# Transposing q and x on TensorE in place of transposing transfers, in a linear-attention and GELU kernel

## The chip, the cores and the metric

The kernel runs on one core of one Trainium2 chip. The core has TensorE (PE, matmuls; its weight loads are listed as PEld), VectorE (DVE), ScalarE (ACT), GpSimd (POOL) and SyncE (SP), which here only issues transfers. The metric is device time in microseconds (us) of one execution, as the median of several runs. Matmuls write to PSUM, which is handed out in banks; everything else that the kernel keeps on the chip lies in SBUF.

## What is computed

For 8 batches, 8 heads, 576 rows and a head size of 64, a linear attention; then two matrix products with a GELU between them.

```python
phi = lambda t: np.where(t > 0, t, np.exp(t) - 1.0) + 1.0
q_p, k_p = phi(q), phi(k)                       # 8 x 8 x 576 x 64
kv = einsum('bhsd,bhse->bhde', k_p, v); z = sum(k_p, axis=2)
x = einsum('bhsd,bhde->bhse', q_p, kv) / (einsum('bhsd,bhd->bhs', q_p, z)[..., None] + 1e-6)
h = x.transpose(0, 2, 1, 3).reshape(4608, 512) @ w_in      # w_in 512 x 2048
out = gelu_tanh(h) @ w_out                                 # w_out 2048 x 512
```

All inputs and the output are fp32 in HBM; on the chip q, k and v become bf16, x, the weights and the GELU's result g fp16.

## The kernel before

**Groups.** The 4,608 rows are worked on in nine groups of 512, `iteration(j)` at line 1065. Group j, from 0 to 7, has the first 512 rows of batch j; group 8 has the remaining 64 rows of each of the eight batches. While group j's matrix products run, the attention of group j+1 is made and the inputs of later batches are mapped.

**Order by hand.** What is issued when is written out in nine lists of words, ORDER_A to ORDER_I (lines 1123 to 1182, group 0 to 8), which `iteration` reads from left to right. Each engine and each queue works through its own instructions in that order. The words:

- `p6` makes block 6 (128 of the 2,048 columns) of h as four plain matmuls of 128x512, and `g6` its GELU. `X`, `Y`, `Z`, `W` with a name are steps of a unit of seven products (`Quad`, line 989): four blocks of h made as seven products of half-size quarters (28 matmuls of 128x256, line 999) in place of eight (16 matmuls of 128x512, line 356). The other steps of a unit are copies and sums: `s` and `u` copy on ACT, `m` copies on DVE, `c` and `a` add on DVE, `g11` to `g22` are GELUs. A prime at a word takes the other of DVE and ACT for its copy. The units' first rows are FIRST_BLOCK = (0, 2, 4, 6) for X, Y, Z, W; X covers blocks 0, 1, 8 and 9.
- A unit needs sums of quarters of w_in (`sum_w_in`, line 956, words `!w0` to `!w3` for X, Y, Z, W; four DVE instructions each) and sums of quarters of x (`sum_x`, word `!xs`).
- `o1` to `o7` with `os`, `ou`, `oc11` and so on make the second product in the same way (line 784), and `S1` to `S4` sum quarters of g on DVE.
- `!lq:3`, `!lk:3`, `!lv:3` issue loads of batch 3 on SP; `!qe`, `!qx`, `!qm` and `!ke`, `!kx`, `!km` make phi of q and k (exp on ACT, the linear part and the minimum on DVE); `!re`, `!rx`, `!rm` do so for the rest rows; `!vc` casts v; `k3` makes kv of batch 3 (line 262).
- `n0` to `n3` make one chunk of 128 rows of the next group's x: matmuls of q's transpose with kv (line 278), then a reciprocal and a multiplication on DVE (lines 295 and 296).

**Transposes.** TensorE needs phi(q) and x with the contracted dimension on the partitions. In groups 0 and 1 both are transposed by TensorE: a transpose is a matmul of 128x128 with the data as weights and an identity as the moving operand, into a PSUM bank, and a copy moves it to SBUF (lines 410, 349, 516, with copies at 413, 350, 521). From batch 2 on, `least_q` (line 619) issues four transposing transfers on SP for each q behind its minimum, `transposed_x` (line 641) issues one for each x chunk behind its division, and `least_rest` (line 565) one for each of the four pieces of the rest rows: `nc.sync.dma_start_transpose`, SBUF to SBUF.

**Buffers.** The pool `pld` has seven load buffers. At the start they are taken by q, k and v of batch 0 and by four blocks of w_in; a later load waits on SP until the readers of an earlier one are done. In group 1 the words `!bq` and `!mq` take two of them for good (tiles A and B), which hold sums of w_out, the sums of w_in for X and W, and small pieces; group 2's `!br` takes one more for rows. Group 0 and group 1 use plain blocks only; group 2 makes two units (Y and Z) and eight plain blocks; groups 3 to 8 make four units. PSUM has a pool of six single banks (`ps_b`) and one pair.

**Around the start.** POOL makes identities, sets constants and casts most of the weights (lines 141 and 147); group 1's maps, transposes and kv are slotted into group 0 by `plan_second` (line 496), `maps` among them.

Of the kernel before, what the change touches and what calls it, by code (L numbers as in the profile page):

```python
# [17 lines left out]
def kernel(  # L18
# [9 lines left out]

# [6 lines left out]
    P = 128  # L39
# [40 lines left out]
    def bank(name, shape, dt=FP32):  # L80
        return ps_b.tile(shape, dt, name=name, tag="b")
# [3 lines left out]

# [65 lines left out]

    nc.scalar.preload_act_table_set("exp_and_others")
# [9 lines left out]
    for i in (2, 1, 3):  # L162
        load_w_in(i)
    load_w_out(0)
# [17 lines left out]

    warm = pg.tile([P, 512], BF16, name="warm", tag="g")
    nc.vector.memset(warm, 0.0)
    ident = pth.tile([P, P], BF16, name="ident")
    make_identity(nc, ident)
    vps = [pkv.tile([P, J * NP, E], BF16, name=f"vp{i}") for i in range(2)]
    ident_x = pth.tile([P, P], FP16, name="ident_x")
    t_sum = pth.tile([P, 3, KM // 2, MAIN // 2], FP16, name="t_sum")
    kvbds = [pkv.tile([P, NP, 2 * E], BF16, name=f"kvbd{b}") for b in range(B)]  # L190
    make_identity(nc, ident_x)
    for i in range(2):
        nc.gpsimd.memset(vps[i][:, :, D:E], 1.0)
    for t in kvbds:
        nc.gpsimd.memset(t, 0.0)

# [4 lines left out]

    phi, exps, own = {}, {}, {}
# [44 lines left out]

# [137 lines left out]
    def xt_chunk(j, c):  # L385
        return xts[j][:, :, P * c : P * (c + 1)]
# [5 lines left out]

# [90 lines left out]

# [12 lines left out]
    def plan_second():  # L496
# [3 lines left out]
        def maps():  # L500
            for n in "qk":
                exp_of(n, b)
            cast_w_out(2, nc.scalar.copy, slice(0, 2))
            linear_of("q", b)
            sum_w_out(slice(0, 1))
            linear_of("k", b)
            for n in "qk":
                least_of(n, b)
# [56 lines left out]
    def least_rest(m):  # L565
        least_of("qr", m)
        if m == 0:
            qts[B] = pt.tile([P, C, NP, P], BF16, name="qt")
        nc.sync.dma_start_transpose(
            out=qts[B][:, m], in_=phi["qr", m][:, 0].rearrange("p h d -> p (h d)")  # L570
        )
# [5 lines left out]
    def load_rests(i):  # L577
# [32 lines left out]
        "bq": lambda j: begin_sums(),  # L610
        "mq": lambda j: more_sums(),
# [7 lines left out]
    def least_q(b, cs=slice(0, C)):  # L619
        least_of("q", b, cs=cs)  # L620
        if b not in qts:
            qts[b] = pt.tile([P, C, NP, P], BF16, name="qt")
        for c in range(cs.start, cs.stop):
            nc.sync.dma_start_transpose(
                out=qts[b][:, c],
                in_=phi["q", b][:, c].rearrange("p h d -> p (h d)"),
            )
# [13 lines left out]
    def transposed_x(b, c, x):  # L641
        if b not in xts:
            xts[b] = pt.tile([P, NP, MAIN], FP16, name="xt")
        nc.sync.dma_start_transpose(out=xt_chunk(b, c), in_=x)

    x_parts = {}

    def attention_piece(b, c, in_banks=False):

        if b < B:  # L650
            return transposed_x(b, c, (nab_in_banks if in_banks else nab)(qts[b], b, c))
# [27 lines left out]
        transposed_x(b, c, x)  # L679
# [36 lines left out]


# [205 lines left out]
    FIRST_BLOCK = (0, 2, 4, 6)  # L923
    def sums_at(u, t):
        own["sums"][u] = t.rearrange("p (u n c) f -> p u n c f", u=1, c=KM // 2)
        own["w"][u] = own["sums"][u][:, 0]

    own["w"], own["sums"] = {}, {}
    for u in (1, 2):
        sums_at(u, w_near[:, u])  # L930

    def begin_sums():

        own["A"] = pld.tile([P, MM + 2, N2], FP16, name="w_sum", tag="ld")
        sums_at(3, own["A"][:, MM // 2 : MM])

    def more_sums():

        own["B"] = pld.tile([P, MM + 2, N2], FP16, name="w_more", tag="ld")
        own["qr", 0] = own["B"][:, MM:].rearrange("p a n -> p (a n)").bitcast(BF16)  # L940
        sums_at(0, own["B"][:, MM // 2 : MM])

# [122 lines left out]
    def iteration(j):  # L1065
# [10 lines left out]
        for word in ORDERS[j].split():  # L1076
# [27 lines left out]
            elif kind == "k":  # L1104
                kv_in_pair(int(name))
            elif kind == "S":
# [4 lines left out]
            elif kind == "!":  # L1111
                what, _, b = name.rstrip("'").partition(":")
                if what == "vc":
                    cast_v_of(int(b), name.endswith("'"))
                elif b:
                    prepare_of[what](int(b))
                else:
                    prepare[what](j)
# [5 lines left out]
        "p0 g0 p1 g1 p2 g2 p3 g3 p8 g8 p9 g9 p10 g10 p11 g11 !w1 p4 g4 p5 g5 p6 g6 p7 g7 p12 g12 "  # L1124
        "p13 g13 p14 g14 p15 g15 !w2 @15 o0:0-4 o1:0-4 o2:0-4 o3:0-4 o0:4-8 o1:4-8 o2:4-8 o3:4-8 "
        "@23 o0:8-10 o1:8-10 o2:8-10 o3:8-10 @27 o0:10-12 o1:10-12 @29 o2:10-12 o3:10-12 o0:12-16 "
        "@32 o1:12-16 @33 !qe:2 o2:12-16 @34 o3:12-16 @35"
    )
    ORDER_B = (
        "p0 !ke:2 p13 !lk:3 p1 !kx:2 !vc:2' !km:2 !t !qx:2 @2 p7 !qm:2 p2 g0 !bq !lv:3 !mq g1 g2 "  # L1130
        "p3 g3 k2 !a0 !a2 !a3 p6 p4 p5 p8 g4 p11 g5 !kxb:3 p9 g6 g7 T0-8 o1 os' g8 g9 p10 !qx:3 "
        "!kxa:3 g10 p12 o7 !lk:4 g11 p14 g12 g13 om S1:0-6 p15 S2:0-5 g14 g15 n1' o2 S1:6-8 "
        "S2:5-8 S4:0-6 n0 oc11' o6 !qe:3 n3' ou S4:6-8 !ke:3 n2 o5 oc22 !lq:4 !km:3 !vc:3 o4 oc21 "
        "o3 oc12' !qm:3 !ke:4 !xs !kx:4"
    )
    ORDER_C = (
        "!br k3 @1 Y1 Z1 !km:4 p6 Zs p0 !lk:5 !t g6 !lv:4 Z2 Zg11 Z6 p14 Z7 p8 Zu Z5 Zm g14 p7 g0 "
        "g8 Ys p15 !qx:4 Zc g7 Y6 Yu' Zg22 Y2 Yg11 Y7 Ym Z4 Za g15 n1 p1 g1 Y5 Yc Zg21 Y4 Ya Z3 "
        "Zg12 S1:4-8 n3 o1 Yg22 S2:4-8 p9 S1:0-1 S2:0-1 n2 Yg21 os g9 Y3 Yg12 S1:1-3 S1:3-4 "
        "S2:1-3 S2:3-4 S3:0-8 !qe:4 n0' o2 !lv:5 !qm:4 o6 oc11 ou o7 om o5 !kx:5 S4:0-8 oc22 "  # L1140
        "!ke:5 !vc:4 !xs o4 oc21 o3 !km:5 k4 oc12"
    )
    ORDER_D = (
        "!lq:5 !w0 Z1 X1 !t Y7 Y1 Xs X2 !w3 X7 @1 Ym' X6 Xg11 Ys n1 Xm' Y2 X4 Y6 Xu Xa X5 Yg11 Zs "
        "Xc Yu Xg21 n0 !lk:6 Y4 !vc:5' Z6 Zu X3 Xg12 Z2 Ya Y5 W1 Z7 Yc Zg11 Ws k5 Xg22 Zm Yg21 W6 "
        "Wu' Z5 Yg22 Y3 Yg12 !lv:6 Zc W7 Wm' W2 Z4 Za W5 Zg22 Z3 Wc W4 Wa n3 Wg11 Zg12 Zg21 o1 "
        "S1:0-6 Wg21 n2 os W3 Wg12 S2:0-6 !lq:6 Wg22 S1:6-8 S2:6-8 o2 !qe:5 S3:0-5 o6 S3:5-8 o7 "
        "S4:0-8 !qx:5 ou !qm:5 om !ke:6 oc11 o5 !lk:7 oc22 !vc:6 !kx:6 o4 o3 oc21 !xs oc12'"
    )
    ORDER_E = (  # L1150
        "X1 X7 Xm Xs Y7 !t X6 X2 Xg11 Xu' @1 Y1 Ym X4 X5 Ys Xa Xg21 Z1 Y2 Yg11 Zs !lr:0 Y4 Xc X3 "
        "!km:6 Y6 Yu n2 Z7 Xg12 Z6 Ya Z2 Zu Xg22 Yg21 n1 Zm W1 Z5 Y5 Yc Zc Zg11 Ws k6 Z4 Yg22 W7 "
        "Za Z3 Wm' Zg22 W6 Wu' n3 W4 Zg12 W2 Wg11 Wa Y3 W5 Wc Yg12 S1:0-6 S2:0-6 Zg21 Wg21 o1 os "
        "n0 Wg22 W3 Wg12 S1:6-8 S2:6-8 S3:0-8 !qx:6 o2 !lv:7 S4:0-8 !qe:6 o6 ou !lq:7 oc11 o7 om "
        "!xs o5 oc22 !re:0 o4 !re:1 !ke:7 !qm:6 oc21 !kx:7 o3 oc12'"
    )
    ORDER_F = (
        "!t !km:7 X1 Y1 Y7 !vc:7' Xs Ym' X6 X7 @1 X2 Xu Y4 Xm' !lr:1 X5 Xc X4 Xa Xg11 Ys k7 Y6 "
        "Yu' Y2 Xg22 Xg21 X3 Z1 Yg11 Zs !qx:7 Y5 W1 Yc Z2 Xg12 Ya Zg11 Z6 Zu Ws' Y3 Z7 Zm n1 Yg12 "
        "Z5 Yg22 W6 Wu S1:0-2 W7 Z4 W2 W5 Wm' Zc !rx:0 Zg22 Z3 Zg12 Wc Wg11 n0 Wg22 W4 S1:2-6 "  # L1160
        "S3:0-6 W3 Wg12 o1 os S1:6-8 S3:6-8 S2:0-8 n3 !qe:7 o7 om' o6 Wa Za Zg21 Yg21 ou' n2 o4 "
        "!qm:7 S4:0-6 o5 oc22 Wg21 o2 !rm:0 oc11 S4:6-8 o3 oc21 oc12 !xs"
    )
    ORDER_G = (
        "X1 n0 !rx:1 !rm:1 Xs Y7 Ym' X7 Xm' X2 X6 Xu' Xg11 Y1 Ys X4 Xa n2 X5 Y2 Z1 Xg21 Y6 Y4 "
        "Yg11 Zs W1 Xc Xg22 Yu' Ya !rx:2 X3 Xg12 Yg21 Y5 @1 Z6 Yc Z2 Z7 Zg11 Zu' Ws' Y3 Z5 Yg22 "
        "W7 Wm' W2 Wg11 Yg12 Zm Zc W6 Wu' W4 Zg22 Wa Z3 Zg12 Z4 W5 Za Zg21 Wc S1:0-6 o1 Wg21 "
        "S2:0-6 os n1 W3 Wg22 Wg12 S1:6-8 S2:6-8 S3:0-8 n3' o2 !rx:3 o6 o7 oc11' !re:2 ou S4:0-8 "
        "om o5 !re:3 !rm:2 oc22 o4 oc21 !rm:3 o3 !xs oc12' !t"
    )  # L1170
    ORDER_H = (
        "X1 Xs X7 Xm' n0' n1 X6 Xu X2 Xg11 X4 Y1 Xa X5 Y7 Xc Ys Y6 Xg21 Y2 Yg11 Yu' Z1 X3 W1 Zs "
        "Y5 Z6 Z2 Xg12 Ym Yc Y4 @1 Z7 Zu' Z5 Xg22 Zg11 Ya Y3 Ws W6 W2 Zm Yg21 Zc W7 Yg22 Wu' Wm "
        "Zg22 Wg11 Z3 Zg12 W5 Z4 Za Yg12 Zg21 Wc Wg22 W4 Wa S1:0-6 o1 os W3 Wg21 S2:0-6 Wg12 "
        "S1:6-8 S2:6-8 S3:0-8 n2 n3' o2 oc11 o6 ou o7 om o5 S4:0-8 o4 oc22 !xs o3 oc21 oc12'"
    )
    ORDER_I = (
        "X1 Y7 Ym X7 Xm Xs X2 Xg11 @1 X6 Y1 X4 Z1 Ys Y6 Xu' Xa Xg21 Y2 Y4 Yg11 Zs X5 Yu' Ya Y5 "
        "Yg21 Z7 Z2 Z6 W1 Xc Xg22 Zg11 Yc Y3 Yg22 Zu' X3 Ws' Z5 W6 Zm Zc Yg12 Wu W2 W7 W5 Wg11 Wm "
        "Zg22 Wc Xg12 Z4 Za Z3 Zg12 W4 Wa W3 Wg12 S1:0-6 S2:0-1 Wg22 o1 S1:6-8 S2:1-8 S3:0-8 o5 "  # L1180
        "Zg21 o6 Wg21 S4:0-8 o7 o2 o4 o3"
# [36 lines left out]
```

## Time and profile before

| what | value |
|---|---|
| median of 3 runs | 265.94 us (265.37 to 266.69) |
| the profiled execution | 266.18 us |
| its span, first to last instruction | 264.4 us |
| last matmuls | from 248.73 us on, 12.24 us |
| transposing transfers | 28 of x, 24 of q, 4 of the rest rows |
| median from issue to landing of these | x 2.3, q 4.1, rest 2.3 and 3.1 us |
| HBM read, written | 36.70 MB, 9.44 MB |

How to read what follows: a line by shape gives line, engine, operation, tiles and shape, then how often it ran, its busy time in us, the mean ns of one, and the idle time of its engine just before. A line of the timeline gives start and length in us, engine, line, operation and count; matmuls are pipelined, so a run's length is a little more than count times spacing. A line of waits gives who waited for whom: us in total, times, longest. A line of sums by stretches gives the stretch, its length and, for each engine, busy us and the number of instructions, then the granted clock, the DMA share and GB/s. Groups begin on PE at about 47.4 (group 1), 77 (group 2), 104, 130.4, 156.8, 183, 208.4 and 234.4 us (group 8).

### The profile page before, as it was taken

The numbers are of one execution on the slowest core, as the hardware profiler recorded it, in microseconds if no ns is written. First come the engines' busy times: TensorE is split into PE (matmuls) and PEld (weight loads), VectorE is DVE, ScalarE is ACT, GpSimd is POOL, SyncE is SP. The second block draws the span as 40 slices with busy tenths as digits, with TensorE's granted clock in tenths as the row PEclk, the third lists the DMA queues.
The fourth block names the chain that finished last, engine by engine and source line by source line (L and its number), as shares of the span: only waits on it lengthen the run. The fifth ranks groups of instructions, "written<-read, shape, count | busy, mean of one in ns | idle before, by whom it ended". The sixth has DMA issues, their size and how long they took to land. (4 is left out here: it accounts for less than half of the span.)

```text
span 264.4 us, 6675 instructions
## 1 busy us (share of the span) xinstructions
PE 257.3 (97%) x2765; PEld 203.0 (77%) x2765; DVE 227.7 (86%) x384; ACT 192.1 (73%) x279; POOL 18.8 (7%) x28
## 2 busy tenths in 40 slices
PE   8999999999999999999999999999999999989994
PEld 2584446446876788888888888989889888878883
DVE  3966497799989999999999999999999788868972
ACT  4768795955988788988898988884876478408810
POOL 8056501000000000000000000000000000000000
PEclk9999999999999999999999999999999999999999
DMA  6999999997969969999697398415620450112004
GB/s 235 402 405 397 409 409 396 407 304 217 222 152 286 327 112 222 346 261 241 191 264 195 57 347 236 82 40 68 174 102 21 126 134 2 24 57 121 2 0 159
DMA packets 59789, 53.90 MB, mean 204 GB/s; under 512 B 35696, under 2 KB 45936, under 8 KB 59760
## 3 DMA queue, kind: packets, MB, share of 16 engines
q1 hardware_dynamic: 56880, 44.57, 58.4%
q10 hardware_dynamic: 2880, 8.91, 9.4%
q8 instruction: 21, 0.34, 0.5%
q14 instruction: 8, 0.07, 0.1%
HBM read 36.70 MB, written 9.44 MB: 175 GB/s over the span
## 5 line engine op out<-in xcount | busy, mean ns | idle before, releaser
L784 PEld LDWEIGHTS <-g 128*128 128x128 f16 x624 | 60.5, 98 | 7.8 <-issue 0.4
L784 PE MATMUL o_ps<-w_out_sb,g 128*128 128x256 f16 x384 | 45.7, 273 | 0.0
L356 PE MATMUL h_ps<-xt,w_in_sb 128*128 128x512 f16 (+2 forms) x212 | 37.3, 327 | 0.0
L999 PEld LDWEIGHTS <-w_in_sb 128*128 128x128 f16 x312 | 30.1, 98 | 5.3 <-issue 1.5
L1014 ACT ACTIVATE g<-hq_ps 128x512 f16<-128x512 f32 x52 | 30.9, 622 | 3.9 <-DVE hq_ps L1027 2.5
L356 PEld LDWEIGHTS <-w_in_sb 128*128 128x128 f16 x212 | 18.0, 98 | 14.8
L784 PEld LDWEIGHTS <-s 128*128 128x128 f16 x272 | 26.5, 98 | 3.5
L376 ACT ACTIVATE g<-h_ps 128x512 f16<-128x512 f32 x40 | 22.2, 604 | 8.6 <-PE h_ps L356 8.3
L296 DVE TENSOR_TENSOR xs<-n_ps,r 128x512 f16<-128x512 f32 (+1 forms) x43 | 25.5, 592 | 1.5
L999 PEld LDWEIGHTS <-w_near 128*128 128x128 f16 x224 | 21.6, 98 | 3.5
L999 PE MATMUL hq_ps<-t_sum,w_near 128*128 128x256 f16 x168 | 24.1, 273 | 0.0
L1027 DVE TENSOR_TENSOR rows<-hq_ps,rows 128x512 f32<-128x512 f32 x26 | 17.6, 685 | 1.9 <-PE hq_ps L999 1.2
L1033 ACT COPY h_ps<-hq_ps 128x512 f32<-128x512 f32 x23 | 13.1, 571 | 8.2 <-PE hq_ps L999 7.7
L905 DVE TENSOR_TENSOR o_sb<-o_ps,o_sb 128x512 f32<-128x512 f32 (+1 forms) x21 | 13.3, 636 | 6.5 <-PE o_ps L784 3.6
L1027 DVE TENSOR_TENSOR hq_ps<-hq_ps,rows 128x512 f32<-128x512 f32 x26 | 17.8, 694 | 1.3 <-PE hq_ps L999 0.7
L230 ACT ACTIVATE k_e<-k_x 128x2304 bf16<-128x2304 f32 (+1 forms) x9 | 17.2, 1913 | 2.2 <-DVE o_sb L905 1.3
L1014 ACT ACTIVATE g<-rows 128x512 f16<-128x512 f32 x26 | 17.0, 652 | 2.4 <-DVE rows L1027 2.3
L1014 ACT ACTIVATE g<-h_ps 128x512 f16<-128x512 f32 x26 | 16.1, 621 | 3.2 <-PE h_ps L999 2.9
L230 ACT ACTIVATE q_e<-q_x 128x2048 bf16<-128x2048 f32 (+1 forms) x9 | 15.5, 1721 | 2.8 <-DMA q_x<-in_q_dram 2.8
L999 PE MATMUL h_ps<-xt,w_in_sb 128*128 128x256 f16 x104 | 15.6, 272 | 1.1 <-ACT h_ps L1033 1.0
L999 PE MATMUL hq_ps<-w_sum,w_in_sb 128*128 128x256 f16 x104 | 15.4, 272 | 0.0
L784 PE MATMUL o_ps<-w_sum,s 128*128 128x256 f16 x128 | 15.3, 273 | 0.0
(113 smaller groups left out, 456.2 us busy)
## 6 DMA issues: line engine op xcount, KB each, us to landing
out_dram<-o_sb ACTq DMA_DIRECT2D x16, 512.0 KB, 3.8
k_x<-in_k_dram SPq DMA_DIRECT2D x7, 1152.0 KB, 9.2
v_x<-in_v_dram SPq DMA_DIRECT2D x7, 1152.0 KB, 9.2
q_x<-in_q_dram SPq DMA_DIRECT2D x6, 1024.0 KB, 9.1
w_st<-in_moe_w_in_dram SPq DMA_DIRECT2D x3, 1024.0 KB, 13.4
q_x<-in_q_dram SPq DMA_DIRECT2D x4, 512.0 KB, 11.6
w_st<-in_moe_w_out_dram SPq DMA_DIRECT2D x2, 1024.0 KB, 12.6
w_st<-in_moe_w_out_dram SPq DMA_DIRECT2D x4, 512.0 KB, 11.1
```

The source lines that it names most:

```text
L230: nc.scalar.activation(o, i, AF.Exp)
L296: nc.vector.tensor_tensor(x_v, n_v[heads + (slice(0, D),)], r[heads + (None,)].to_broadcast(shape + [D]), op=ALU.mult,)
L356: nc.tensor.matmul(h_ps[:, ts], lhsT=w_in_sb[:, c, P * m : P * (m + 1)], rhs=xt[:, c, ts], start=(c == 0), stop=(c == KM - 1), skip_group_ ...
L376: nc.scalar.activation(g_v, h_v, AF.Gelu_apprx_tanh)
L784: nc.tensor.matmul(ps[t] if type(ps) is list else ps[:, t, :], lhsT=lhs[:, m, P * t : P * (t + 1)], rhs=rhs[:, m, :], start=(first and m = ...
L905: nc.vector.tensor_tensor(out, i0, i1, op=ALU.add)
L999: nc.tensor.matmul(ps[:, f], lhsT=lhs[:, c, P * f : P * (f + 1)], rhs=rhs[:, c], start=(first and f == 0 and c == 0), stop=(c == KM // 2 - 1),
L1014: nc.scalar.activation(g_v, src, AF.Gelu_apprx_tanh)
L1027: add = lambda out, i0, i1: nc.vector.tensor_tensor(out, i0, i1, op=ALU.add)
L1033: on(nc.scalar.copy, nc.vector.tensor_copy)(self.seed, self.b)
```

## The change

From batch 2 on, q, the rest rows and x are transposed by TensorE in place of transfers. New words place each step: `!qta:b` and `!qtb:b` transpose the two halves of batch b's q, 8 transposes each and a copy of 1,024 elements; `!rt:m` a piece of the rest rows, 4 transposes and a copy of 512; `t0` and `t1` the two halves of the next group's x, 8 transposes each and a copy of 1,024. A prime puts the copy on DVE, else it is on ACT. `!qm`, `!rm` and `n0` to `n3` no longer issue transfers.

Tiles A and B are taken from the load buffers right behind the first block loads of w_in. All four sets of sums of w_in are made in group 0: `!w0` stands behind `!w1` in its list and W's set is called in `maps`. The words `!bq`, `!mq`, and group 3's `!w0` and `!w3` are gone. Group 2 makes three units, X, Y and Z, and four plain blocks (6, 7, 14 and 15).

The setup of constants stands ahead of the loads in the text; its instructions are the same, but two memsets of POOL on A and B are added behind the loads' issue.

All nine lists but the first few words of group 0's are written anew. The new words in them, with their primes:

| group | q | rest | x of the next group |
|---|---|---|---|
| 1 | `!qta:2'` `!qtb:2` `!qta:3` `!qtb:3'` | | `t0'` `t1'` |
| 2 | | | `t1` `t0` |
| 3 | `!qta:4'` `!qtb:4'` | | `t0` `t1` |
| 4 | `!qta:5'` `!qtb:5'` `!qta:6'` | | `t1'` `t0` |
| 5 | `!qtb:6'` `!qtb:7'` | | `t0` `t1'` |
| 6 | `!qta:7'` | `!rt:0'` `!rt:1'` `!rt:3'` | `t0'` `t1` |
| 7 | | `!rt:2` | `t1` `t0` |

The diff, cut to what matters (of the lists only group 2's):

```diff
+    own = {"w": {}, "sums": {}}
+    FIRST_BLOCK = (0, 2, 4, 6)
+    def sums_at(u, t):
+        own["sums"][u] = t.rearrange("p (u n c) f -> p u n c f", u=1, c=KM // 2)
+        own["w"][u] = own["sums"][u][:, 0]
+    def tiles_of_sums():
+        for n in "AB":
+            own[n] = pld.tile([P, MM + 2, N2], FP16, name="w_" + n, tag="ld")
+            nc.gpsimd.memset(own[n][:, 0, 0:2], 0.0)
+        own["qr", 0] = own["B"][:, MM:].rearrange("p a n -> p (a n)").bitcast(BF16)
+        for u, t in enumerate((own["B"][:, MM // 2 : MM], w_near[:, 1], w_near[:, 2])):
+            sums_at(u, t)
+        sums_at(3, own["A"][:, MM // 2 : MM])
...
+    tiles_of_sums()
...
+            sum_w_in(3)
...
     def least_rest(m):
         least_of("qr", m)
-        if m == 0:
-            qts[B] = pt.tile([P, C, NP, P], BF16, name="qt")
-        nc.sync.dma_start_transpose(
-            out=qts[B][:, m], in_=phi["qr", m][:, 0].rearrange("p h d -> p (h d)")
-        )
...
-        "bq": lambda j: begin_sums(),
-        "mq": lambda j: more_sums(),
...
     def least_q(b, cs=slice(0, C)):
         least_of("q", b, cs=cs)
-        if b not in qts:
-            qts[b] = pt.tile([P, C, NP, P], BF16, name="qt")
-        for c in range(cs.start, cs.stop):
-            nc.sync.dma_start_transpose(
-                out=qts[b][:, c],
-                in_=phi["q", b][:, c].rearrange("p h d -> p (h d)"),
-            )
...
-    def transposed_x(b, c, x):
+    def copied(other):
+        return nc.vector.tensor_copy if other else nc.scalar.copy
+    def transpose_q_half(b, s, other):
+        if b not in qts:
+            qts[b] = pt.tile([P, C, NP, P], BF16, name="qt")
+        t_ps = bank("t_ps", [P, 2, NP, P], BF16)
+        for c in range(2):
+            for i in range(NP):
+                nc.tensor.transpose(
+                    t_ps[:, c, i, :], phi["q", b][:, 2 * s + c, 2 * i : 2 * i + 2, :], ident
+                )
+        copied(other)(qts[b][:, 2 * s : 2 * s + 2], t_ps)
+    def transpose_rest(m, other):
+        if m == 0:
+            qts[B] = pt.tile([P, C, NP, P], BF16, name="qt")
+        t_ps = bank("t_ps", [P, NP, P], BF16)
+        for i in range(NP):
+            nc.tensor.transpose(t_ps[:, i, :], phi["qr", m][:, 0, 2 * i : 2 * i + 2, :], ident)
+        copied(other)(qts[B][:, m], t_ps)
+    def transpose_x_half(b, s, other):
         if b not in xts:
             xts[b] = pt.tile([P, NP, MAIN], FP16, name="xt")
-        nc.sync.dma_start_transpose(out=xt_chunk(b, c), in_=x)
+        t_ps = bank("t_ps", [P, NP, 2, P], FP16)
+        for c in range(2):
+            for i in range(NP):
+                x = chunks[b, 2 * s + c][:, P * i : P * (i + 1)]
+                nc.tensor.transpose(t_ps[:, i, c, :], x, ident_x)
+        copied(other)(
+            xts[b][:, :, 2 * P * s : 2 * P * (s + 1)], t_ps.rearrange("p i c n -> p i (c n)")
+        )
+    transpose_of = {
+        "qta": lambda b, other: transpose_q_half(b, 0, other),
+        "qtb": lambda b, other: transpose_q_half(b, 1, other),
+        "rt": transpose_rest,
+    }
+    chunks = {}
     x_parts = {}
     def attention_piece(b, c, in_banks=False):
         if b < B:
-            return transposed_x(b, c, (nab_in_banks if in_banks else nab)(qts[b], b, c))
+            chunks[b, c] = (nab_in_banks if in_banks else nab)(qts[b], b, c)
+            return
...
-        transposed_x(b, c, x)
+        chunks[b, c] = x
...
+            elif kind == "t":
+                transpose_x_half(j + 1, int(name[0]), name.endswith("'"))
...
-                if what == "vc":
+                if what in transpose_of:
+                    transpose_of[what](int(b), name.endswith("'"))
+                elif what == "vc":
...
     ORDER_C = (
-        "!br k3 @1 Y1 Z1 !km:4 p6 Zs p0 !lk:5 !t g6 !lv:4 Z2 Zg11 Z6 p14 Z7 p8 Zu Z5 Zm g14 p7 g0 "
-        "g8 Ys p15 !qx:4 Zc g7 Y6 Yu' Zg22 Y2 Yg11 Y7 Ym Z4 Za g15 n1 p1 g1 Y5 Yc Zg21 Y4 Ya Z3 "
-        "Zg12 S1:4-8 n3 o1 Yg22 S2:4-8 p9 S1:0-1 S2:0-1 n2 Yg21 os g9 Y3 Yg12 S1:1-3 S1:3-4 "
-        "S2:1-3 S2:3-4 S3:0-8 !qe:4 n0' o2 !lv:5 !qm:4 o6 oc11 ou o7 om o5 !kx:5 S4:0-8 oc22 "
-        "!ke:5 !vc:4 !xs o4 oc21 o3 !km:5 k4 oc12"
+        "Z1 @1 !br Z7 !t p14 p6 Zs' Z2 g6 Zg11 !kx:4 Zm Y1 Z6 p7 g14 !lv:4 !lr:0 Z4 Ys g7 Y7 Y6 "
+        "!km:4 Y2 Ym' Zu' Z5 Yu Za Zg21 Y4 Yg11 p15 Zc Z3 !qx:4 Ya X1 g15 Xs' Zg22 Zg12 k3 Y5 Yc "
+        "Yg21 X6 X7 Xu n1 X2 Xm' Xg11 Yg22 X5 Xc Xg22 n2' X4 Xa n3 Y3 Yg12 X3 Xg12 S1:0-8 S2:0-8 "
+        "Xg21 o1 os !vc:4 t1 n0 !qe:4 o2 S3:0-8 S4:0-8 o6 ou' !lk:5 k4 !kx:5 t0 !xs o7 o5 om o4 "
+        "!ke:5 oc22 oc11 oc21 o3 !qm:4 oc12'"
```

## The prediction

> **What bounds the kernel now.** I read the page's busy shares and slices first, then sums by stretches, then the timeline at a transpose that TensorE already makes, then instructions by shape, and last the waits. The page:
>
> ```profile
> PE 257.3 (97%) x2765; PEld 203.0 (77%) x2765; DVE 227.7 (86%) x384; ACT 192.1 (73%) x279; POOL 18.8 (7%) x28
> ...
> PEclk9999999999999999999999999999999999999999
> ```
>
> TensorE (PE) is busy 97% of the span at full granted clock. But matmul ends are modelled, so a busy PE could hide slow issue. The chain that ended last tests that: it ends in one run of 112 matmuls of 128x256 in 12.24 us, 109.3 ns each, in a stretch where DMA is nearly idle.
>
> ```profile
> 248.73 12.24 PE o_ps L784 x112
> ```
>
> Where DMA is busiest the timeline has 16 such matmuls in 1.91 us (from 59.20 us on, line 784), the last of them 0.273 us long: (1.91 - 0.273) / 15 = 109.1 ns. The same pace: PE isn't stretched by transfers. Sums by stretches, groups 2 to 5 (us; PE, PEld, DVE, ACT, POOL busy):
>
> ```profile
> 77.00:104.00 27.00, 27.00 (x292) 21.05 (x287) 26.34 (x47) 22.66 (x30) 0.00 (x0) 1.00 0.98 248
> 104.00:130.40 26.40, 26.06 (x325) 22.77 (x314) 25.67 (x44) 23.68 (x36) 0.00 (x0) 1.00 1.02 251
> 130.40:156.80 26.40, 26.36 (x315) 23.32 (x313) 25.64 (x45) 22.97 (x34) 0.00 (x0) 1.00 0.74 207
> 156.80:183.00 26.20, 26.14 (x310) 22.84 (x308) 25.43 (x42) 20.17 (x31) 0.00 (x0) 1.00 0.49 124
> ```
>
> PE idles 0.45 us in these 106 us, VectorE (DVE) 2.9 us. PE sets the pace; DVE is close behind, so DVE's added work has to be counted too.
>
> **Part 1: transposes on PE (added).** Group 1's q is already transposed by PE, between matmuls of group 0:
>
> ```profile
> 36.33 0.81 PE L709 MATMUL o_ps<-w_out_sb,g 128*128 128x512 f16 x3
> 36.98 1.06 PE L516 MATMUL t_ps<-ident,q_p 128*128 128x128 bf16 x16
> 37.87 0.59 PE L709 MATMUL o_ps<-w_out_sb,g 128*128 128x512 f16 x2
> ```
>
> From the first transpose's start to the next matmul's start 37.87 - 36.98 = 0.89 us pass for 16: 0.056 us of PE time each. The weight loads (97 ns each) are overlapped, as before every other matmul. New ones: x of groups 2 to 8, two halves of 8 each, 7 x 16 = 112; q of batches 2 to 7, 6 x 16 = 96; the rest rows, 4 x 4 = 16. Together 224 x 0.056 = **+12.5 us** on the engine that has no room. The idle that could hide some of it is the shortfall of PE in the stretches: 0.45 us above and 0.57 us from 47.4 to 77 us (29.03 busy of 29.60), about 1.0 us; after 183 us only 0.05 us to 234.4.
>
> A rule speaks against this change more sharply than my row does. The Trainium skill, "TensorE: Matmul & The Clock Gate", section "Part 4: PE-mode transpose", gives about 275 ns for such a transpose inside a kernel and says that the clock gate doesn't count transposes as activity. By it, as an estimate, 224 x 0.275 = 61.6 us would be added, some 328 us in all. Here the row shows a duration of 219 ns but a spacing of 56 ns, and the granted clock stays 1.00 across it; new runs are of 4 or 8, shorter than this one of 16. I go by the spacing.
>
> **Part 2: group 2's third unit (removed).** Four plain blocks of four 128x512 matmuls go; one unit of 28 matmuls of 128x256 comes. The plain spacing is (5.35 - 0.379) / 23 = 0.216 us (24 in 5.35 us from 54.01 on, line 356). So 28 x 0.1093 - 16 x 0.216 = 3.06 - 3.46 = **-0.4 us** of PE.
>
> **Part 3: copies of the transposes out of PSUM (added).** By the primes in the new lists: 12 q halves and 14 x halves of 1,024 elements, 15 on DVE and 11 on ScalarE (ACT); four rest pieces of 512, three on DVE. Their rows:
>
> ```profile
> L521 ACT COPY qt<-t_ps 128x1024 bf16<-128x1024 bf16 x2 | 1.9, 1015 | 0.3 <-PE t_ps L516 0.3
> ...
> L350 DVE COPY xt<-t_ps 128x512 f16<-128x512 f16 x2 | 0.8, 425 | 0.4 <-PE t_ps L349 0.4
> ```
>
> ACT: 11 x 1.015 + 0.59 = 11.8 us. DVE has no 1,024-element row of this copy: it is bounded by 0.425 and 0.85 (twice the 512 row). Sums of 16-bit data (line 744) take 418 ns at 512 and 686 at 1,024, so I add 0.268 to the 0.425: 0.69. DVE: 15 x 0.69 + 3 x 0.425 = 11.7 us (7.7 to 14.0). The new unit adds about three DVE instructions of 0.69 (its s, c and a words: 2.1 us) and two ACT copies of 0.59 (1.2 us). DVE becomes 227.7 + 13.8 = 241.5 us, ACT 205 us. In a span of some 278 us that is 87% and 74%, as now: beside PE, not on the path, as long as it is spread. From 77 to 183 us, words of groups 2 to 5: DVE gets 9 half copies (6.2) and the unit (2.1), and loses the sums of part 4 (3.3): +5.0 us. PE gets 15 halves x 8 x 0.056 - 0.4 = +6.3 us. So DVE's share falls a little there. Only group 2 by itself is tight: DVE +2.1, PE +0.9 - 0.4 = +0.5, DVE idle now 0.66, which leaves 0.95 us that a neighbouring group must take.
>
> **Part 4: sums of w_in (moved).** Words w0 and w3 leave group 3, where their eight instructions take DVE from 105.18 to 108.44 us, 3.3 us. They go to group 0. There DVE idles 3.3 us in one piece before line 730 waits for POOL (from 30.0 us), and 2.1 us before the second of the sums already made there. In group 0 a sum beside a POOL cast took 1.99 us instead of 0.42 (line 969, two of eight), so eight cost 3.3 to at most 16 us; nearest is one slow one in four, as in the two sets now made there: 3.3 + 2 x 1.57 = 6.4 us, into 16.27 busy of 22.40. Queued behind them on DVE are group 1's maps and casts, then the first sum of w_out, which waits for POOL until 33.25 anyway. Cost on the path 0; without that cover group 1's transposes and kv would slip, by 6.4 - 5.4 = 1 us.
>
> **Part 5: load buffers (moved).** Tiles A and B hold two of the seven from the start, so the loads of w_out and of batches 1 and 2 share five, each waiting on SP for an earlier reader. By the readers' ends: w_out's first block waits for v's cast, 12.4 us (issued at 12.10 now); k of batch 2 for the exp of batch 1's k, 36.3 (33.71 now). DMA is backed up all through group 0 (1.06 busy share from 25 to 47.4 us), so an issue 0.3 to 2.6 us later still finds a queue ahead of it. POOL's two tiny memsets wait for the first q and k buffers, free by about 10 us, before POOL's first cast at 13.03. Cost 0; at worst batch 2's k and v land 2.6 us later, and PE waits for them (0.52 us at 53.30 now).
>
> **Part 6: transfers (removed).** 56 transposing transfers leave SP's queue, each 1.19 us or more there and 2.3 to 7.5 us to landing, and SP's long waits for xs and q_p go with them; loads behind them issue earlier. But the only wait for such a transfer on a compute engine over 0.2 us is DVE's:
>
> ```profile
> DVE t_sum L987 <- DMA xt<-xs: 1.4, 1, 1.4
> ...
> PE h_ps L999 <- ACT h_ps L1033: 1.0, 2, 0.8
> ```
>
> It doesn't stand on PE. Gain: 0.
>
> **Part 7: new order and hand-overs (unknown).** PE now waits for nothing but PSUM banks and copies. Thirty new hand-overs (transpose, copy, bank free) take banks from the six-bank pool. Below: a better order could give back the idle of 1.0 us. Above: each costs 0.5 us, the mean of the two waits in the last row shown: 15 us. Nearest is what all copies of that line cost: 26 hand-overs, 1.0 us in sum, 0.04 each. So 30 x 0.04 = **+1.2 us**.
>
> **The sum,** against the profiled execution, 266.18 us (span 264.4, and 1.8 around it): 266.2 + 12.5 - 0.4 + 1.2 = 279.5. The median of the three runs is 265.94, 0.24 lower: **279.2 us**, 5% slower. Within 0.5% is about what a measurement of this kernel can't tell from no change.
>
> **Rivals.**
> A, PE count alone: the order hides every hand-over and takes back the idle: 279.2 - 1.2 - 1.0 = 277.0; I treat 276 to 281 as my forecast's case. Chance 0.66.
> B, DVE's queue: a copy that PE needs stands behind one or two DVE instructions, and DVE is 97% busy in groups 2 to 5. If the 18 DVE copies cost 0.2 to 0.5 us each in place of 0.04, that is +2.9 to +8.3 us, with group 2's 0.95 up to 9.2: 282 to 288. For: DVE's 2.9 us of idle in 106. Against: its share falls a little. Chance 0.25.
> C, five load buffers starve groups 0 and 1: +2.6 us for batch 2 and as much again for batch 3's k: 284, or more if the DMA queue runs dry. For: SP issues wait for readers already. Against: the backlog. Chance 0.06.
> D, the other side: the transfers' latency is the limit. Each group's x goes divide, transfer (2.3 us), sums, products; PE's path is 0.45 + 0.69 us, 1.16 us shorter. If each of the seven group starts waited for that transfer, 7 x 1.16 = 8.1 us would go, and the transposes would sit in the holes: 265.9 - 8.1 - 0.4 = 257. It decides only where PE idles at least 16 x 0.056 = 0.9 us per group for x alone; the stretches show 0.57 us at most, and no PE wait on DMA. Chance 0.02. That the PE transposes are not what costs (another 0.01 for no change) needs PE room, which is not there.
>
> **Numbers.** Range 276 to 285.5: below, the PE count with all idle given back (277.0) less 0.4% for the spread of runs; above, into B's upper half and past C. Faster 0.02, same 0.01, slower 0.97.
>
> **What would show it.** Transposes at lines of transpose_q_half and transpose_x_half spaced 0.056 us; PE busy 12 us more; each of groups 3 to 7 about 1.8 us longer (32 transposes x 0.056), group 2 only 0.5 to 1.5; no DMA_TRANSPOSE on SP; DVE near 241, ACT near 205 us. Wrong if the transposes' spacing is near 0.1 us or more, if PE waits for t_ps copies sum to over 3 us, or if PE idles in groups 0 and 1 behind loads.

## The result and the profile after

The changed kernel takes 277.85 us (four runs, 277.71 to 278.0); the kernel before took 266.06 us on the same chip. The ratio is 1.0444, 95% interval 1.0417 to 1.0471: 4.4% slower, +11.8 us. 279.2 us was predicted, with a range of 276 to 285.5.

The page of the changed kernel (busy us, share of the span, instructions; then the granted clock by slices):

```profile
PE 268.9 (97%) x3000; PEld 216.4 (78%) x3001; DVE 242.4 (88%) x394; ACT 203.4 (74%) x292; POOL 18.9 (7%) x30
...
PEclk9999999999999999999999999999999999999999
```

PE grew by 11.6 us and the span by 11.5 (264.4 to 275.9): PE is as full as it was. DVE was worked out at 241.5 and ACT at 205; they have 242.4 and 203.4. A transposing run in the changed kernel's timeline, and by shape the copies out of its banks:

```profile
99.99 0.62 PE L664 MATMUL t_ps<-ident_x,xs 128*128 128x128 f16 x8
100.44 1.25 PE L812 MATMUL o_ps<-w_out_sb,g 128*128 128x256 f16 x10
```

```profile
L665 ACT COPY xt<-t_ps 128x1024 f16<-128x1024 f16 x9 | 9.0, 1008 | 1.7 <-PE t_ps L664 1.7
...
L647 DVE COPY qt<-t_ps 128x1024 bf16<-128x1024 bf16 x10 | 6.8, 685 | 0.9 <-PE t_ps L644 0.8
...
L665 DVE COPY xt<-t_ps 128x1024 f16<-128x1024 f16 x5 | 3.4, 682 | 0.0
```

Eight transposes hold PE from 99.99 to 100.44 us, 0.056 each. The DVE copy that had no row before takes 0.685 us; 0.69 was estimated. Sums by stretches, groups 2 to 5 of the changed kernel (their products end at 107.59, 135.92, 164.34 and 192.33 us):

```profile
79.10:107.59 28.49, 28.46 (x390) 23.78 (x389) 26.94 (x44) 24.74 (x34) 0.00 (x0) 1.00 0.54 172
107.59:135.92 28.33, 28.27 (x348) 25.05 (x346) 27.24 (x48) 24.36 (x34) 0.00 (x0) 1.00 0.54 183
135.92:164.34 28.42, 28.31 (x347) 25.12 (x345) 27.33 (x44) 23.94 (x36) 0.00 (x0) 1.00 0.31 106
164.34:192.33 27.99, 27.99 (x347) 25.19 (x345) 26.93 (x47) 20.93 (x33) 0.00 (x0) 1.00 0.29 98
```

PE idles 0.20 us in these 113 us, less than the 0.45 in 106 before. DVE idles 4.8 us. The chain of the changed kernel ends in the same 112 matmuls, in the same 12.24 us:

```profile
260.24 12.24 PE o_ps L812 x112
```

Adding up, by shape, the time from each matmul's start to the next gives the books of both traces (us, worked out from the starts):

```
shape and kind                    before    after    change
128x128 (transposes, pieces of h)   7.45    19.99    +12.54
128x256 (units, second product)   180.09   182.82     +2.72
128x512 (plain blocks)             44.83    41.75     -3.08
128x512 warm-up                    10.52    10.24     -0.27
128x130, 64x65, 128x384            16.62    16.21     -0.41
sum                               259.50   271.01    +11.50
```

The 224 transposes account for +12.54, exactly 0.056 each. Units against blocks are 28 x 0.109 - 16 x 0.216 = -0.40 by count and spacing; their two rows sum to -0.36, but waits are in them too. What is neither, so all waits and hand-overs together, is 11.50 - 12.54 + 0.40 = -0.64, and its sign is minus.

### The profile page after: what moved, and what is told of

The parts are those of the page before. It is cut to its first block, busy times and chain, and to the rows that moved or that the text cites. A ratio compares the mean times of both kernels' runs of the same rounds, so it can differ in the third digit from the quotient of the medians.

```text
span 275.9 us, 7052 instructions
## 1 busy us (share of the span) xinstructions
PE 268.9 (97%) x3000; PEld 216.4 (78%) x3001; DVE 242.4 (88%) x394; ACT 203.4 (74%) x292; POOL 18.9 (7%) x30
## 4 chain that ended last, share of the span: by engine, by line
PE 81%; DVE 7%; DMA 5%; ACT 3%; SPq 1%; issue 1%; POOL 1%; ACTq 0%
PE o_ps L812 31%; PE hq_ps L1007 25%; PE h_ps L365 5%; DMA w_st<-in_moe_w_in_dram 5%; PE h_ps L812 4%; PE h_ps L1007 4%; PE n_ps L287 2%; PE t_ps L664 2%; PE o_ps L739 2%; PE kv_ps L271 2%; DVE w_B L977 2%; PE t_ps L644 2%; DVE w_near L977 2%; DVE w_A L977 1%; ACT k_e L240 1%
## 5 line engine op out<-in xcount | busy, mean ns | idle before, releaser
L1007 PEld LDWEIGHTS <-w_in_sb 128*128 128x128 f16 x324 | 31.0, 98 | 5.0 <-issue 1.1
L1022 ACT ACTIVATE g<-hq_ps 128x512 f16<-128x512 f32 x54 | 31.7, 619 | 4.3 <-PE hq_ps L1007 2.1
L365 PE MATMUL h_ps<-xt,w_in_sb 128*128 128x512 f16 (+2 forms) x196 | 33.8, 322 | 0.2 <-ACT g L385 0.2
L365 PEld LDWEIGHTS <-w_in_sb 128*128 128x128 f16 x196 | 16.3, 98 | 13.4 <-issue 0.5
L385 ACT ACTIVATE g<-h_ps 128x512 f16<-128x512 f32 x36 | 20.0, 603 | 4.8 <-PE h_ps L365 4.7
L1022 ACT ACTIVATE g<-h_ps 128x512 f16<-128x512 f32 x27 | 16.7, 620 | 4.6 <-PE h_ps L1007 4.4
L1035 DVE TENSOR_TENSOR rows<-hq_ps,rows 128x512 f32<-128x512 f32 x27 | 18.4, 686 | 1.6 <-PE hq_ps L1007 0.9
L1007 PE MATMUL h_ps<-xt,w_in_sb 128*128 128x256 f16 x108 | 16.2, 272 | 0.8 <-ACT h_ps L1041 0.6
L1007 PE MATMUL hq_ps<-xt,w_in_sb 128*128 128x256 f16 x108 | 16.2, 273 | 0.0
L1007 PE MATMUL hq_ps<-w_A,w_in_sb 128*128 128x256 f16 x108 | 16.0, 272 | 0.0
L1041 ACT COPY h_ps<-hq_ps 128x512 f32<-128x512 f32 x19 | 10.9, 572 | 6.3 <-PE hq_ps L1007 5.7
```

What stands on the lines that cost most here:

```text
L365: nc.tensor.matmul(h_ps[:, ts], lhsT=w_in_sb[:, c, P * m : P * (m + 1)], rhs=xt[:, c, ts], start=(c == 0), stop=(c == KM - 1), skip_group_ ...
L385: nc.scalar.activation(g_v, h_v, AF.Gelu_apprx_tanh)
L1007: nc.tensor.matmul(ps[:, f], lhsT=lhs[:, c, P * f : P * (f + 1)], rhs=rhs[:, c], start=(first and f == 0 and c == 0), stop=(c == KM // 2 - 1),
L1022: nc.scalar.activation(g_v, src, AF.Gelu_apprx_tanh)
L1035: add = lambda out, i0, i1: nc.vector.tensor_tensor(out, i0, i1, op=ALU.add)
L1041: on(nc.scalar.copy, nc.vector.tensor_copy)(self.seed, self.b)
```

## The experiments

Two theories stood against each other. **PE theory:** PE has no room, so 224 x 0.056 us come on top and little else matters. **DVE theory:** DVE is so full that the copies and its queue set the addition. A third, the order theory, gives part of it to the new lists, the buffers and the moved sums. Ratios below are to the kernel before on the same chip; other differences, unless the text says otherwise, are to the changed kernel's 277.8 us, which it had on two chips (277.85 and 277.76), not on those of every run below, so a few tenths of a microsecond between runs mean little.

### Transposes twice

```diff
-        for c in range(2):
+        for c in (0, 1, 0, 1):
...
-        for i in range(NP):
+        for i in 2 * list(range(NP)):
```

> The changed kernel (277.85 us) with each of its 224 new transposes issued twice into the same bank; copies, lists and buffers as they are. PE theory (PE has no room, and a transpose takes 0.056 us of it): +224 x 0.056 = +12.5 us, 290.4 us, between 289.5 and 291.5. DVE theory (the addition comes from the copies and from DVE's full queue): PE has room, less than +4 us, under 282. If a transpose cost more than its spacing shows, by the duration of 0.219 us, +49 us, 327.

289.38 us, ratio 1.0889 (1.0864 to 1.0915): +11.6 us on the changed kernel, for 12.5 of PE work. Sums by stretches show PE without a hole:

```profile
48.00:78.00 30.00, 30.00 (x324) 21.20 (x321) 26.84 (x36) 23.56 (x31) 0.00 (x0) 1.00 0.74 279
78.00:108.00 30.00, 30.00 (x428) 25.51 (x426) 27.49 (x45) 26.35 (x34) 0.00 (x0) 1.00 0.49 158
```

PE work added is paid almost in full, and at the spacing, not at the duration of 0.219 us.

### DVE copies twice

```diff
+        def twice(out, in_):
+            for _ in range(2):
+                nc.vector.tensor_copy(out, in_)
-        return nc.vector.tensor_copy if other else nc.scalar.copy
+        return twice if other else nc.scalar.copy
```

> The changed kernel with each of the 18 DVE copies out of the transposes' banks made twice; PE's work is the same, DVE gets 15 x 0.69 + 3 x 0.42 = 11.6 us more, 9 x 0.69 = 6.2 us of it in groups 2 to 5, where DVE idles about 4.5 us in 113. PE theory: DVE is near its limit but not at it, so +0 to +3 us, 278 to 281. DVE theory: the copies are what the change costs, so twice the copies cost as much again, +8 to +12 us, 286 to 290.

284.19 us, ratio 1.0694 (1.0669 to 1.0719): +6.4 us, between the two. The PE theory as I had stated it (0 to 3) falls here: of 11.6 us of added copies a little under half stayed out of the time. The waits of this run name DVE where PE stands:

```profile
PE n_ps L287 <- DVE qt L638: 1.4, 2, 0.7
...
PE hq_ps L1011 <- DVE t_sum L999: 1.2, 1, 1.2
...
PE hq_ps L1011 <- DVE qt L638: 0.7, 1, 0.7
```

Two things are mixed in this: a copy made twice also lands later for the matmul that needs it. From 77 to 208 us DVE idles 3.9 us while PE idles 4.8, so DVE's lack of room isn't shown to be all of the 6.4 us.

### x's transposes at half their PE time

This kernel leaves the transposition of x out: two matmuls with the identity as weights fill each bank.

```diff
-        for c in range(2):
-            for i in range(NP):
-                x = chunks[b, 2 * s + c][:, P * i : P * (i + 1)]
-                nc.tensor.transpose(t_ps[:, i, c, :], x, ident_x)
+        for c in range(2):
+            nc.tensor.matmul(
+                t_ps[:, 256 * c : 256 * (c + 1)],
+                lhsT=ident_x,
+                rhs=chunks[b, 2 * s + c][:, 0:256],
...
```

> The changed kernel with x not transposed: each of the 14 x halves fills its bank by two matmuls of 128x256 with the identity as weights (2 x 0.109 = 0.218 us of PE) in place of eight transposes (8 x 0.056 = 0.448); the copies, their waits and everything else stay, and the products work on wrong values. It leaves the transposition of x out. PE theory: -14 x 0.23 = -3.2 us against the changed kernel, that is 8.6 us above the kernel before on the same chip (8 to 9.2). If DVE already sets the time as much as PE does (copies made twice cost 6.9 us): less than half of it comes, 10.2 us or more above before.

276.45 us, 9.9 above before (ratio 1.037, 1.0349 to 1.0391), and 1.3 below the changed kernel on the same chip (277.76). The bounds that I had set miss both ways, 9.2 and 10.2; against the changed kernel less than half of the 3.2 us came. PE's starts show where the rest went: the 112 transposes' 6.27 us are gone, the 28 new matmuls stand 0.109 us apart as planned (3.05), but the time from start to start at 128x256 rose by 4.66, so some 1.6 us is new waiting. PE work added is paid almost in full, PE work taken away is won back by less than half, so something stands close behind PE. What it is, this run doesn't show: the list of waits names only two new ones of PE, 0.26 and 0.16 us, both for copies on ACT, and none for DVE.

### All transposes back on transfers, in the new lists

```diff
+        for c in range(cs.start, cs.stop):
+            nc.sync.dma_start_transpose(
+                out=qts[b][:, c],
+                in_=phi["q", b][:, c].rearrange("p h d -> p (h d)"),
+            )
...
-            chunks[b, c] = (nab_in_banks if in_banks else nab)(qts[b], b, c)
+            transposed_x(b, c, (nab_in_banks if in_banks else nab)(qts[b], b, c))
...
-                    transpose_of[what](int(b), name.endswith("'"))
+                    pass
```

> The changed kernel with all transposes back on transfers, issued where the kernel before issues them (behind q's minimum, behind each x chunk's division); its new lists, its load buffers, group 0's sums and group 2's third unit stay. PE theory: -12.5 us, 265.3 us, or up to 2 us more where a list now expects x 1 us after its division and the transfer takes 2.3: 265 to 267.5. Order theory (a good part of the 11.8 us comes from the new lists, the two load buffers taken early or the sums in group 0): 268 to 275. DVE theory: DVE loses 11.6 us and ACT 11.8, so also near 265; this run doesn't tell it from the PE theory, the two above do.

297.4 us, ratio 1.1205 (1.1163 to 1.1248): 19.5 us slower than the changed kernel, though it has 12.5 us less of PE work. All three expectations fall. PE is 89% busy, with waits of 7.8, 6.9, 4.0 and 2.7 us between matmuls' starts. The longest, 7.8 us, starts in SP's queue, as its timeline shows (start, length, queue, line, operation), and ends at DVE:

```profile
112.13 6.39 SPq L630 DMA_TRANSPOSE qt<-q_p  x4
118.62 0.53 SPq L90 DMA_DIRECT2D v_x<-in_v_dram  x1
```

```profile
124.25 1.36 DVE L260 CAST vp<-v_x 128x2304 bf16<-128x2304 f32 x1 [9.24 <-DMA v_x<-in_v_dram]
```

v of batch 5 stands in the new lists right behind q's minimum of batch 4. In the changed kernel, with no transfer ahead of it, it is issued at 97.73 us; behind four transposing transfers, which wait for that minimum and then take SP 6.4 us, it is issued at 118.62 us. DVE works in order, so its cast of v blocks it for 9.24 us, and with it the sums that PE waits for. Behind the other three waits DVE stands as well, each time for something else:

```profile
154.67 0.76 DVE L1012 TENSOR_TENSOR t_sum<-xt 128x512 f16<-128x512 f16 x2 [5.79 <-DMA xt<-xs]
106.66 1.36 DVE L248 TENSOR_SCALAR k_p<-k_x 128x2304 bf16<-128x2304 f32 x1 [3.63 <-DMA k_x<-in_k_dram]
80.06 0.76 DVE L1012 TENSOR_TENSOR t_sum<-xt 128x512 f16<-128x512 f16 x2 [3.82 <-DMA xt<-xs]
```

The wait of 6.9 us is x's own transfer: it leaves SP at 145.84 us, right behind two loads, and lands at 154.57, 8.7 us later, where 2.3 is the median in the kernel before. The wait of 4.0 us is a load again: k of batch 5 leaves at 100.52 us, behind x's transfers, in place of 82.35. In the wait of 2.7 us x's last transfer stands in SP's queue behind the four of q and leaves at 76.56 us.

### q and the rest rows alone on transfers

The first half of the edit above is made, and the transposition of x stays on PE.

> The changed kernel with q and the rest rows back on transfers and x on PE: 112 of the 224 transposes go, and with them 13 of the 18 DVE copies (9.6... by rows 10 x 0.69 + 3 x 0.42 = 8.2 us of DVE) and 3 of the 12 ACT copies. PE theory: half of 12.5, -6.3 us, 271.6 us (271 to 272.5), as PE work goes by halves. DVE theory: by DVE's share of the copies, 8.2 of 11.6, -8.8 us of the 12.5, 269.

288.42 us, ratio 1.0844 (1.0796 to 1.0891), +10.6 on the changed kernel. The same place is caught more plainly: v of batch 5 is issued at 97.73 us in the changed kernel, and here at 113.46, behind four transfers of q that begin at 108.15. PE waits 8.5 us for it (by way of DVE):

```profile
97.73 0.37 SPq L90 DMA_DIRECT2D v_x<-in_v_dram  x1
```

```profile
108.15 5.19 SPq L630 DMA_TRANSPOSE qt<-q_p  x4
113.46 0.50 SPq L90 DMA_DIRECT2D v_x<-in_v_dram  x1
```

```profile
119.27 1.36 DVE L260 CAST vp<-v_x 128x2304 bf16<-128x2304 f32 x1 [10.24 <-DMA v_x<-in_v_dram]
122.55 1.01 PE L1019 MATMUL hq_ps<-xt,w_B 128*128 128x256 f16 x4 [8.50 <-DVE rows L1047]
```

### x alone on transfers

The other half of that edit is made, and q stays on PE.

> The changed kernel with x on transfers, and q and the rest rows on PE. PE theory by count alone: 112 transposes less, -6.3 us, 271.6. Queue theory: SP's transfers of x wait for divisions through the middle of each group and hold up the loads behind them, as q's did in the run that took 288.4 us: 282 to 292. Latency theory: x's sums follow its halves closely in the new lists, +2 us in each of seven groups, less 6.3: about 285 with PE waits at each group's start and none for loads.

288.76 us (285.14 to 289.8; the slowest of the four is the one profiled), ratio 1.0799 (1.0714 to 1.0885). PE's long waits are 4.8 us at 105.1 and 3.8 at 143.9 us. In front of both DVE stands, once for a load and once for x:

```profile
106.33 1.36 DVE L248 TENSOR_SCALAR k_p<-k_x 128x2304 bf16<-128x2304 f32 x1 [4.47 <-DMA k_x<-in_k_dram]
145.45 0.76 DVE L1000 TENSOR_TENSOR t_sum<-xt 128x512 f16<-128x512 f16 x2 [4.62 <-DMA xt<-xs]
```

The load, k of batch 5, leaves SP at 99.33 us behind four transfers of x (82.35 in the changed kernel). The transfer of x leaves at 137.80, right behind two loads, and lands at 145.43, 7.6 us later. So the longer wait fits the queue theory and the shorter one the latency theory, with a latency that is three times the median of 2.4 us.

### The loads moved to POOL's queue

```diff
-        nc.sync.dma_start(out=ld[name, b][:, us, :], in_=s[:, us, :])
+        (nc.sync if b < 3 else nc.gpsimd).dma_start(out=ld[name, b][:, us, :], in_=s[:, us, :])
...
```

These lines load k and v. For q the same is done from batch 4 on, and for all rest rows.

> The changed kernel with all transposes back on transfers, as in the run that took 297.4 us, and the loads of batches 3 to 7 (k, v), 4 to 7 (q) and of the rest rows issued by POOL, which is idle from 45 us on, so that SP's queue has transposing transfers only. Queue theory (that run's long waits come from loads that stand on SP behind transfers that wait for DVE; its longest wait was DVE's 9.2 us for v): the waits go, 265 to 269 us. Latency theory (the new lists use a transpose so soon after its source that 2.3 us or more of a transfer show each time): 280 or more, as PE still waits for xt and qt.

303.72 us, ratio 1.1414 (1.1361 to 1.1466): slower still. DVE waits 10.8 us for q of batch 3 until 66 us (one wait), and PE 10.5 us behind it; PE waits another 10.5 us for sums of x, for which DVE waits 11.9. Neither is mainly a blocked queue. q of batch 3, still on SP, leaves at 40.31 us as in the changed kernel (40.80), but lands at 65.96 in place of 53.22, while k of batch 3, which POOL issued at 43.70, lands at 53.05. And x's last transfer stands 3.6 us behind four of q, leaves at 88.78 us and lands at 100.02. POOL's queue is then held up in order as SP's was, for buffers (k of batch 4 left at 55.50 us, q of batch 4 at 69.03, after a wait of 12.78 us). So with two queues the long waits are late landings; what slows them, this run doesn't show.

### The kernel before with its transposes on PE

The code of the new transposes, and new words put into the old lists by a plain rule, for instance in group 1:

```diff
-        "p0 !ke:2 p13 !lk:3 p1 !kx:2 !vc:2' !km:2 !t !qx:2 @2 p7 !qm:2 p2 g0 !bq !lv:3 !mq g1 g2 "
-        "p3 g3 k2 !a0 !a2 !a3 p6 p4 p5 p8 g4 p11 g5 !kxb:3 p9 g6 g7 T0-8 o1 os' g8 g9 p10 !qx:3 "
+        "p0 !ke:2 p13 !lk:3 p1 !kx:2 !vc:2' !km:2 !t !qx:2 @2 p7 !qm:2 p2 g0 !bq !lv:3 !mq g1 g2 "
+        "p3 !qta:2' g3 k2 !a0 !a2 !a3 p6 !qtb:2' p4 p5 p8 g4 p11 g5 !kxb:3 p9 g6 g7 T0-8 o1 os' "
```

> The kernel before with nothing changed but the transposes: the 224 go to PE, and the new words are put into its old lists by a plain rule (q's halves two and four PE words behind the minimum, x's halves three PE words behind the last chunk of the half, q copies on DVE, x copies on ACT). Load buffers, sums and group 2 as before. PE theory: 266.06 + 12.5 = 278.6 us and what a rule-made place costs in waits, 278.5 to 283. Lists theory (PE's transposes fit only with lists written for them, as transfers did not fit into the new lists): over 285.

294.9 us, ratio 1.1072 (1.1027 to 1.1118): 28.6 us above the kernel before; 12.5 of it is PE work, and the other 16, by subtraction, are waits and what they bring. The first long one, from the timeline, is PE in front of batch 2's first transposes:

```profile
55.81 0.62 PE L638 MATMUL t_ps<-ident,q_p 128*128 128x128 bf16 x8 [2.92 <-DVE q_p L246]
```

A transfer that waits for q's minimum holds up SP's queue. A transpose in PE's queue that waits for it holds up every matmul behind it. The changed kernel pays only 11.8 us in all; it differs from this run by its lists, buffers and moved sums together, so how much of that is due to the lists alone isn't shown.

### W's sums back in group 3

```diff
-            sum_w_in(3)
...
-        "!t !lv:5 X1 ...
+        "!t !w3 !lv:5 X1 ...
```

> The changed kernel with one call moved: W's sums of w_in are made at the start of group 3, where the kernel before makes them, in place of group 0's maps. In the changed kernel one of these four took 1.99 us beside a POOL cast, the minimum of q slipped, and PE waited 0.62 us before group 1's transposes. If that wait is on the path: -0.6 us, 277.2, as long as group 3's DVE has room for 1.5 us. If DVE has none there (it idles about 1 us in that group): +0 to +1, 277.9 to 278.8.

279.11 us, ratio 1.0485 (1.0447 to 1.0523), +1.3 us, or +1.1 by ratio, with intervals that overlap (the changed kernel has 1.0444, 1.0417 to 1.0471); all four times, 278.9 to 279.64, lie above all of the changed kernel. The wait of 0.62 us in group 0 was worth less than 1.5 us of DVE in group 3: there the copy of q's transposes slips behind the sums, and PE stands for its bank:

```profile
112.98 0.61 PE L643 MATMUL t_ps<-ident,q_p 128*128 128x128 bf16 x8 [1.07 <-DVE qt L646]
```

Three more new waits of PE, 0.9 us together, stand in group 1, at 64.7, 68.6 and 71.2 us. Their cause was not followed.

### Group 2 with two units

X's seven products in the new list of group 2 are replaced by plain blocks (`X1` by `p0`, `Xs'` by `g0`, `X6` by `p8`, `Xu` by `g8` and so on; X's other words go).

> The changed kernel with group 2's third unit undone: X's words give way to plain blocks 0, 8, 1 and 9 in the same places. PE theory: +16 x 0.216 - 28 x 0.1093 = +0.4 us, 12.2 us above the kernel before on the same chip. DVE theory: three DVE instructions of 0.69 us go from the group where DVE has the least room, so -0.5 to -1.5 us, 10.3 to 11.3 us above.

278.04 us, ratio 1.0429 (1.0407 to 1.0451); the changed kernel beside it 277.76 (1.0419). +0.3 us where 0.4 was worked out, though the intervals overlap. It is no gain, so DVE's three instructions aren't the limit there.

### Warm-up by transposes

```diff
-        keep_warm(18)
+        tw_ps = bank("tw_ps", [P, 4, P], BF16)
+        for i in range(72):
+            nc.tensor.transpose(tw_ps[:, i % 4, :], warm[:, 0:P], ident)
```

> The changed kernel with its first 18 warm-up matmuls of 128x512 replaced by 72 transposes of 128x128 of the same zeros. In the changed kernel the warm-up matmuls start 0.427 us apart and, from about 6.5 us on, 0.216 us apart. If transposes count as activity for the granted pace, they go from about 0.107 us apart to 0.056 after some 5 us, and what follows keeps its pace. If they don't (the rule that my prediction weighed), they stay 0.107 us apart to the end, and the transposes of q behind them do too. The time moves by less than 2 us either way, as the start waits for loads.

277.75 us in a single run. The 72 transposes take 6.58 us and start 0.106 to 0.107 us apart until 6.43 us, from there on 0.055 to 0.057, and q's transposes behind them keep that:

```profile
1.36 6.58 PE L425 MATMUL tw_ps<-ident,warm 128*128 128x128 bf16 x72 [1.36 <-POOL ident masks.py:199]
7.77 0.61 PE L418 MATMUL t_ps<-ident,q_p 128*128 128x128 bf16 x8
```

Transposes alone bring PE to its full pace, 5.1 us after the first of them; in the changed kernel the warm-up matmuls get there at 7.1 us, 5.9 us after their first. This run alone doesn't exclude that the pace changes with time alone; the last section shows PE back at half pace after idling.

### The changed kernel once more

> The changed kernel as it is, once more, beside the three others on one chip, so that differences of a few tenths can be read against it: 11.8 us above the kernel before (11.5 to 12.1) under every theory.

277.76 us, 11.2 us above before (ratio 1.0419, 1.0397 to 1.044), a little under what I expected: the kernel before had 266.53 us on this chip, the changed one the same as elsewhere.

## Why the prediction was right, and where its size was off

- **What bounds it:** right, but too simple. PE has no room (twice the transposes: +11.6 us). DVE is nearer to the limit than I took it to be (DVE copies twice: +6.4 us of 11.6), though part of that can be that the copies land later.
- **Part 1, transposes:** 12.5 us worked out, 12.54 in the starts. The row decided rightly against the rule of the Trainium skill, "TensorE: Matmul & The Clock Gate", "Part 4: PE-mode transpose". Its 0.275 us each, taken as the cost, would by that estimate have made some 328 us; here 0.219 us is how long one lasts, and 0.056 what it costs. That transposes don't count as activity isn't so here: in the warm-up they alone halve their spacing at 6.43 us.
- **Part 2, the unit:** -0.4 worked out, +0.3 us when undone, with overlapping intervals. That the starts give -0.36 is luck: waits of +0.4 in the row of plain blocks and -0.3 in that of the units cancel.
- **Part 3, copies:** DVE +14.7 us against 13.8, ACT +11.3 against 13.0, none of it seen on the path as the lists stand: no wait of PE in the list names a copy of the new transposes.
- **Part 4, the sums:** I took 0 on the path and named 1 us if the cover failed. It failed by 0.62 us (from start to start; 0.45 of it shows as idle), by the mechanism named. The timeline of the changed kernel has one of W's four sums at 1.99 us beside POOL's cast, the minimum of q behind it, and PE:

```profile
31.60 1.99 DVE L977 TENSOR_TENSOR w_A<-w_A,w_in_sb 128x512 f16<-128x512 f16 x1
...
36.37 1.22 DVE L256 TENSOR_TENSOR q_p<-q_p,q_e 128x2048 bf16<-128x2048 bf16 x1
```

```profile
37.65 1.07 PE L524 MATMUL t_ps<-ident,q_p 128*128 128x128 bf16 x16 [0.45 <-DVE q_p L256]
```

What I had not weighed is what the move frees: 1.5 us of DVE in group 3. Undoing it for W costs 1.1 to 1.3 us.
- **Part 5, buffers:** 0, as predicted: after 10 us no compute engine but POOL, casting weights, waits over 1 us for a load.
- **Part 6, transfers:** a gain of 0 was taken, from waits on the transfers themselves. What I had not weighed is what they ask of the lists: every load behind them on SP. That is where the longest waits of three of the runs with transfers start, 7.8, 8.5 and 4.8 us; without the transfers the new lists may put a load right behind a minimum. Transfers of x that landed late cost waits beside it.
- **Part 7, hand-overs:** the term that was mis-sized, +1.2 us. The list of waits has a single wait of PE for a copy over 0.5 us:

```profile
PE h_ps L1007 <- ACT h_ps L1041: 0.6, 1, 0.6
```

PE's holes from group 1 to group 7 sum to 1.0 us in both kernels, none at a transpose's bank. All waits and hand-overs came out at -0.64 us in the starts, Part 4's +0.62 included. Without the term the sum would have been 278.0 us; that this is so near to 277.85 has luck in it, as Part 4's +0.62 is offset by waits elsewhere that became 1.26 us shorter.
- **Signs:** PE's growth, the spacing, DVE's and ACT's busy time and group 2 (+1.4 us) came as named. Groups 3 to 7 did not each grow by about 1.8 us: from products' end to products' end it was 0.4, 2.0, 1.3, 2.9 and 1.5, as the new lists also move work between groups: group 3 has 72 of kv's matmuls of 64x65 where it had 136.
- **Rivals:** A it was, at 277.85, though the idle that A takes back is still there (1.0 us in both). B's mechanism is real, as the run with copies made twice shows, but no wait here names such a copy. C and D left no trace.

What stays open: a version with transfers and lists written for the new buffers was not tried, so the share of lists, buffers and sums in the result isn't parted. Of the four long waits with all transposes on transfers, 11.8 us are at loads behind transfers, 6.9 at x's own landing and 2.7 at x behind q; how these share the 19.5 us isn't shown, as PE's slower pace behind three of them comes on top. No kernel here beats the one before.

## What to carry to other kernels

Work moved from transfers to an engine that is full is paid at its issue spacing, not its duration and not by the share of busy time; read that spacing from a place in the trace where the same instruction already stands between others. A hand-written order belongs to the engines and queues it was written for: a transfer that waits holds up the loads behind it, a transpose that waits holds up the matmuls, and exchanging one for the other in a list written for the other cost 16 to 32 us here, PE's own work aside. When two engines are both nearly full, double and halve the work of each before naming the bound.

## What the runs showed of the hardware

After long waits PE comes back at half pace. In the traces here this followed on all nine waits of PE of 3.5 us and more behind the start, for 3.1 to 5.7 us each, and on none of the ten of 1.0 to 2.9 us. In the run with all transposes on transfers it waited from 119.6 to 127.5 us; the granted clock fell to 0.62 and 0.52 (sums by stretches, PE busy, then clock), and 128x256 matmuls stood 0.213 us apart until 130.7 us, 0.109 after:

```profile
123.00:127.50 4.50, 0.00 (x0) 0.62 0.79 283
127.50:131.00 3.50, 3.47 (x17) 0.52 0.06 15
131.00:135.00 4.00, 4.00 (x41) 1.00 0.78 239
```

In that run 47 matmuls of 128x256 ran at this pace; at 0.104 us more each that is an estimated 4.9 us.

At the start of the changed kernel the matmuls stand 0.427 us apart, at half pace too, though the record says 1.00 there (sums by stretches, PE busy, then clock): the spacing is the safer sign.

```profile
2.00:4.00 2.00, 2.00 (x6) 1.00 0.84 251
```
